# Forgetting attention and gated conv FFN on one core: a new written-out order for all engines, with the transposing loads in runs

## Chip, cores and metric

The kernel runs on one core of a Trainium2 chip. The metric is the device time of one execution in microseconds. The kernel before takes 264.0 us, the median of three runs (262.02 to 265.18).

## The reference

The inputs are q, k, v of shape (8, 8, 576, 64), that is batch, heads, sequence and head size, gates f of shape (8, 8, 576), and three weights. Cut to what matters:

```python
scores = scale * q @ k^T
decay  = cum[:, :, :, None] - cum[:, :, None, :]        # cum = cumsum(log(clip(f)))
attn   = softmax(where(causal, -1e9, scores + decay))
x      = (attn @ v), heads side by side                  # (8, 576, 512)
h      = relu(x @ w_in)                                  # (8, 576, 1024)
gate   = sigmoid(3-tap depthwise conv of h along the sequence)
out    = (h * gate) @ w_out                              # (8, 576, 512)
```

## The kernel before

**Attention.** The work goes by half batches of four heads, called hb, 16 of them. Two transposing DMAs (`load_qk`, line 172) bring k and q of one hb into one of four buffers `qk`, each value's two 16-bit halves in neighbouring partitions. The even partitions are then cleared of what isn't used and given rows for the decay: for hb 0 to 5 VectorE does it (`clamp`, line 182) and GpSimd starts small transfers of the rows (`own_rows`, `rows_of`, lines 188 to 199); from hb 6 two ordinary DMAs do both (`fill`, lines 205 and 207). TensorE then computes the scores in three kinds of task: `diag_scores` (diagonal blocks), `off_scores` (the blocks beside the diagonal, line 338) and `tail_scores` (the last 64 columns). ACT takes the exponential of each (`diag_exp`, `off_exp`, `tail_exp`, lines 383, 370, 350), GpSimd applies the causal mask on diagonal and tail blocks (lines 389, 353). `sums` and two `pv` tasks (line 406) give the row sums and the product with v; VectorE inverts the sums (`recip`, lines 414 to 416) and normalises into `xt` (`norm`, line 423).

**FFN.** For each of the 8 batches there are eight column blocks ff: `ffn1` on TensorE (line 433), `relu` on ACT (437), two conv steps on VectorE (443, 445), `tanh` on ACT (448), `gate` on VectorE (452). When all eight gates of a batch are there, `ffn2` (459, 464) multiplies with w_out, ACT copies the result out of PSUM (`evac`, 484) and SP stores it (492, 495). The last batch runs `ffn2_last` (473, 476), block by block as the gates come. FFN of one batch lies among the attention of later ones.

**Loads of ordinary kind.** `load_v` (line 249) brings v of a batch as five DMAs. w_in comes in four quarters (`load_in`, line 228), each cast to 16 bit by ACT (234) or VectorE (236). The first four ff blocks of a batch need the first two quarters only, the last four need all. w_out comes in four parts (`load_out`, 239). All of these, the transposing loads, the fills and the stores are issued by SP, in one order, and share one hardware queue.

**What sets the order.** Each piece is a task with an engine, a duration, the tasks it follows, and the buffers it takes and gives back (`Plan`, from line 12). The order of the tasks on each engine is written out by hand, as one string of letters per engine (`ORDER`, line 655; `KINDS`, line 647, says what a letter means; letters of one kind are taken in the order in which the tasks were added). `Plan.play` (line 36) walks through the five strings with the tasks' assumed durations, so as to merge them into one program order and to give each task its buffer. Buffers: four PSUM tiles `ps`, four `qk`, seven `pp`, two `vf` for v in 32 bit, three `ob` for results (line 112). A load into `qk` of hb n must follow the exponentials of hb n - 4.

The letters needed to follow the text: on TensorE d, o, t are diagonal, off-diagonal and tail scores, s sums, p pv, f ffn1, g and h ffn2, l and m ffn2_last. On VectorE k clamp, c the cast of w_in, r recip, n norm, a and b the conv steps, G gate, E evac. On SP y is load_v, j a quarter of w_in, J a part of w_out, q one transposing load (half of an hb), z fill, S store.

Of the kernel before, what the change touches and what calls it, by code (L numbers as in the profile page):

```python
# [18 lines left out]
class Plan:  # L19
# [11 lines left out]
    def add(self, kind, engine, time, after, fn, take=(), give=(), dma=0.0, small=False, lock=False):  # L31
        self.tasks.append(dict(kind=kind, engine=engine, time=time, after=list(after), fn=fn,
                               take=list(take), give=list(give), dma=dma, small=small, lock=lock))
        return len(self.tasks) - 1
# [50 lines left out]
def kernel(  # L85
# [93 lines left out]
    def clamp(hb, side, c0, c1):  # L179
        t = qk_t[hb % RING].bitcast(U16)[:, 0:2 * HS].rearrange("p (a x) -> p a x", a=2)  # L180
        t = t[:, :, c0:c1] if side is None else t[:, side, c0:c1]
        nc.vector.tensor_scalar(t, t, lim[:, 0:1], 0.0 if apart(hb, c0 // S) else lim[:, 1:2], op0=ALU.mult, op1=ALU.add)  # L182
# [18 lines left out]
    def fill(hb):  # L201
        c = slice(hb * HH, (hb + 1) * HH)
        none = image[3]
        nothing = bass.AP(tensor=none.tensor, offset=int(none.offset), ap=[[2 * S, 60], [1, 2 * HS]])
        nc.sync.dma_start(even_rows(hb, 8, 60, 0, 2 * HS),
                          nothing)
        nc.sync.dma_start(even_rows(hb, 0, 4, 0, 2 * HS).rearrange("j (a x) -> j a x", a=2),
                          image[:, :, c, :].rearrange("j a h s -> j a (h s)"))
# [43 lines left out]
    def cast_v(t_load, t_cast, hb, part, eng):  # L252
        vf, va = vf_t[slot[t_load, "vf"]][:, HH * (hb % 2):HH * (hb % 2 + 1)], va_t[slot[t_cast, "va"]]
        if part == 0:
            eng.tensor_copy(va[:, :, 0:4, :], vf[:, :, 0:4, :])  # L255
        else:
            eng.tensor_copy(va[0:SL, :, 4, :], vf[0:SL, :, 4, :])
# [87 lines left out]
    def tail_scores(me, hb):  # L345
        for h in range(HH):
            scores(ps_t[slot[me, "ps"]], SL * h, hb, h, 512, 512, SL, m=SL)
# [26 lines left out]
    def diag_scores(me, i):  # L374
        for x in range(WARM.get(i, 0) if i else 0):
            nc.tensor.matmul(ps_t[slot[me, "ps"]][:, 0:512], kc[:, 0:128], kc[:, 64:576], start=True, stop=True)
        for s in range(2):
            hb, h = where(i, s)
            for x, m in enumerate(DIAG):
                scores(ps_t[slot[me, "ps"]], 512 * (x // 2) + 256 * s + 128 * (x % 2), hb, h, 128 * m, 128 * m, 128)  # L380
# [48 lines left out]
    def ffn1(me, t_x0, ff):  # L429
        ps, xt = ps_t[slot[me, "ps"]], xt_t[slot[t_x0, "xt"]]  # L430
        for cc in range(NCC):
            for a in range(2):
                nc.tensor.matmul(ps[:, MB + 288 * a:MB + 288 * (a + 1)], w_in_f16[:, cc, 128 * ff:128 * (ff + 1)],  # L433
                                 xt[:, cc, 288 * a:288 * (a + 1)], start=(cc == 0), stop=(cc == NCC - 1))
# [19 lines left out]
    def ffn2(t_o, t_g0, c):  # L454
        ps, hg = ps_t[slot[t_o, "ps"]], hg_t[slot[t_g0, "hg"]]
        if c < 4:
            o = ps[:, 512 * (c % 2):512 * (c % 2 + 1)]
            for ff in range(NFF):
                nc.tensor.matmul(o, hg[:, ff, 128 * c:128 * (c + 1)], w_out_f16[:, ff, :],  # L459
                                 start=(ff == 0), stop=(ff == NFF - 1))  # L460
        else:
            for ff in range(NFF):
                for a in range(2):
                    nc.tensor.matmul(ps[64 * a:64 * (a + 1), 0:256], hg[:, ff, 512:576],  # L464
                                     w_out_f16[:, ff, 256 * a:256 * (a + 1)],
                                     start=(ff == 0), stop=(ff == NFF - 1), skip_group_check=True)
# [45 lines left out]
    for hb in range(NHB):  # L512
# [10 lines left out]
        if hb == 0:  # L523
# [5 lines left out]
            for y in range(2):  # L529
                for x in range(2):  # L530
                    e, d = (("ACT", 0.94), ("DVE", 0.6))[x]
                    t_win.append(add("cast_in", e, d, [t_win[2 * y + x]], lambda me, x=x, y=y, t_x=t_win[x]: cast_in(x, y, t_x),
                                     give=[(("vf", "hg")[x], t_win[x])] if y else [], lock=(e == "DVE")))
        if hb == 3:
            for w in range(4):
# [3 lines left out]
        e, eng, d = ("DVE", nc.vector, (0.7, 0.3)) if b == 0 else ("POOL", nc.gpsimd, (1.12, 0.5))  # L539
        x = add("cast_v", e, d[0], [t_vl[b]], lambda me, hb=hb, b=b, eng=eng: cast_v(t_vl[b], me, hb, 0, eng), take=["va"],  # L540
                lock=True)
# [6 lines left out]
        elif hb == 1:  # L548
            rows, most = [], []
            for s in (1, 0):  # L550
                x = add("clamp", "DVE", 0.46, [t_ld[hb, s]], lambda me, hb=hb, s=s: clamp(hb, s, 0, 2 * S), lock=True)
# [5 lines left out]
        elif hb < NCL:  # L557
            x = add("clamp", "DVE", 1.5, lands, lambda me, hb=hb: clamp(hb, None, 0, HS), lock=True)
            y = add("rows_of", "POOL", 1.2, [x, t_image], lambda me, hb=hb: rows_of(hb), small=True)
            rows = ([x, y],) * 2  # L560
        else:
            x = add("fill", "SP", 1.3, lands + [t_const, t_image], lambda me, hb=hb: fill(hb), dma=2.1)
            rows = ([x],) * 2
        for p in range(2):
            i = 2 * hb + p
            slow = ((3.0, 1.2)[p] if hb < 2 else 1.0)
            if p == (hb < 2):
                x = t_tail[hb] = add("tail_scores", "PE", (0.5 if hb < 2 else 0.2), rows[0] + rows[1], lambda me, hb=hb: tail_scores(me, hb),
                                     take=["ps", "pt"])
# [4 lines left out]
            x = t_dg[i] = add("diag_scores", "PE", 0.46 * slow, rows[p], lambda me, i=i: diag_scores(me, i),  # L574
                              take=["ps", "p"])
# [26 lines left out]
    for b in range(B):  # L602
        for ff in range(NFF):
            ready = [t_norm[4 * b + c] for c in range(4)] + t_win[4:6 if ff < 4 else 8]
            x = add("ffn1", "PE", 0.98, ready, lambda me, b=b, ff=ff: ffn1(me, t_x0[b], ff), take=["ps", "ht"],
                    give=[("xt", t_x0[b])] if ff == NFF - 1 else [])
# [10 lines left out]
        if b == B - 1:  # L617
# [7 lines left out]
            for a in range(3):  # L625
                e, d = (("ACT", 0.92), ("DVE", 1.2), ("ACT", 0.3))[a]
# [7 lines left out]
        for c in range(5):  # L634
# [3 lines left out]
            else:  # L638
                x = add("ffn2", "PE", 1.74, done, lambda me, t_o=t_o, g0=g0, c=c: ffn2(t_o, g0, c))
            t_f2 = x  # L640
            if c in (1, 3, 4):
# [5 lines left out]
    KINDS = {"w": "conv_weights", "d": "diag_scores", "o": "off_scores", "t": "tail_scores", "s": "sums",  # L647
             "p": "pv", "f": "ffn1", "g": "ffn2", "h": "ffn2_end", "l": "ffn2_last", "m": "ffn2_last_end",
             "D": "diag_exp", "O": "off_exp", "T": "tail_exp", "c": "cast_in", "R": "relu", "H": "tanh",
             "C": "cast_out", "E": "evac", "e": "evac_end", "k": "clamp", "W": "conv_ratios", "v": "cast_v",  # L650
             "V": "cast_v_end", "r": "recip", "n": "norm", "a": "conv", "b": "conv_end", "G": "gate",
             "x": "own_rows", "9": "own_row", "M": "diag_mask", "N": "tail_mask", "i": "decay_image",
             "X": "rows_of", "I": "constants", "y": "load_v", "j": "load_in", "q": "load_qk", "J": "load_out",
             "z": "fill", "S": "store"}
    ORDER = {
        "PE": "wdoodotodoosdotpopsppffffdoofdfofodtofdoostdpdopostoppoffffoggfdgtgosfdfopofohdtsdopppooffodfgfd"
              "gotsfffogogtdofppdosoopphodfffdfogtogsofpfofdgotdgpsoofppodftfodfhsfogogftppoffdfdgoosogoppshdof"
              "fdffhogfftogdfogfpdtgopsoopopdsdfofffophtpoffogsfgppgffgfffggfgfgfhfllllllllllllllllmmmmmmmm",
        "ACT": "DOOTODDOOODTOOcRRRHRcHDHOOHDRORODTRHOORHDHOCTDODOTOCHCRRCRORHOHHRDETHEOHRDROOROHeDTDHOHORORORDHH"
               "DRHTOEHRRORHOETDORHDOOOHOHReRDRDRHOHTOEHRORHORDOHDHTEOROHODRTRHODReRHOOHHTERHORRHDDROHHOOOHEeDRR"  # L660
               "DRRHOHOeRHHTRODHROERHDHTOEOOOHDDRORRHROHeTOHRROHREHHRHHRRHREHRERHRHEHRReHHHEe",
        "DVE": "kkWkkvvVVrnncrnnkabaaabbGGkGcbGabkababGranGnbrnnkGGaababGbaGaGbGbrGanbaabbrnnnGGaGabbabGaGbGabaG"
               "rabbnnaGrnbnGGGaabbabaGGbrGnaababGbGnrGnnGabaaGbbraaGbbGGnnaGbaaGbbarbGnGnGraababGaGbbaGbGabaGnb"
               "aGGnrbnnGrabaabbaGGnnGbaabraGnbnGbaGbGGabaGbaGbabGabGabGaaGbbGGE",
        "POOL": "x9MMNiMMNXXMMXNvVMMNvVMNMXIMvNVMvVMNMMMvNVvVMMNvvVVNMMMNMvvVNVMNMMMvvVVMNMMMNvVvVMNM",
        "SP": "yjjqqjqqjqqyJJqqJJqqyqzqqSzySqqzqyzSSqqSqzqyzqSqSSzqqSyzSqqSSzqqyzSSSSSSSSSSSS",
    }
    begin = {"EV": 0.0, "PE": 9.2, "ACT": 9.2, "DVE": 11.6, "POOL": 13.2, "SP": 13.5}
    for number in plan.play({e: [KINDS[x] for x in line] for e, line in ORDER.items()}, begin, 14.4, 6.5):
# [31 lines left out]
```

The softmax here doesn't subtract the row's maximum and nothing guards it: scores larger than these inputs give would overflow.

## Time and profile before

The profiled execution has a span of 265.7 us.

| engine | busy, us | share of the span |
|---|---|---|
| TensorE, matmul | 237.4 | 89% |
| TensorE, weight load | 154.0 | 58% |
| VectorE | 229.2 | 86% |
| ScalarE (ACT) | 203.0 | 76% |
| GpSimd (POOL) | 102.6 | 39% |

The DMA engines moved 49.28 MB, 48.00 MB of it on the one queue that SP fills. The profile's second part cuts the span into 40 equal slices and gives each engine's busy share of a slice in tenths. Its fourth part follows the chain of work that ended last back from the end, and says which engine and line held it for which share of the span; SPq stands for time in which SP issued a DMA. The timeline of SP lists each issue with its start and duration. The windows view gives, for a stretch of time, the busy time of TensorE, its weight loads, VectorE, ACT and POOL (with the number of instructions), then the granted clock of TensorE, the share of the DMA engines and what they moved in GB/s.

### The profile page before, as it was taken

What the parts mean: (1) busy time and instruction counts of PE and PEld (TensorE: products, weight loads), DVE (VectorE), ACT (ScalarE), POOL (GpSimd) and SP (SyncE); (2) the same over time, 40 slices, a digit from 0 to 9 for tenths busy, and PEclk for the clock granted to TensorE, in tenths of its full rate; (3) what the DMA queues carried; (4) which work ended last, traced back from release to release, by engine and by line L of the source; (5) the groups of instructions that cost most, each with busy time, mean ns of one, the idle gap of its engine ahead of it and who ended that gap; (6) DMA issues with size and microseconds to landing.
All of it is one profiled execution on the core that took longest, in us unless ns stands there. A gap on an engine that the chain in (4) does not pass through costs nothing.

```text
span 265.7 us, 7117 instructions
## 1 busy us (share of the span) xinstructions
PE 237.4 (89%) x2937; PEld 154.0 (58%) x2937; DVE 229.2 (86%) x327; ACT 203.0 (76%) x272; POOL 102.6 (39%) x145
## 2 busy tenths in 40 slices
PE   7979862987899997999799999998999999999991
PEld 2557542654565665746566576665766576565641
DVE  6547896678998998798999999999998999989971
ACT  4158465589988997889598998897799998557641
POOL 4248113256445750944705454347117913000000
PEclk9999999599999999999999999999999999999998
DMA  6999999999999999999999999999999920022414
GB/s 139 193 230 213 193 182 208 208 257 159 211 205 235 158 294 192 198 199 211 230 271 225 215 184 289 173 209 235 237 197 174 256 94 2 0 81 84 153 43 179
DMA packets 121895, 49.28 MB, mean 185 GB/s; under 512 B 113735, under 2 KB 114771, under 8 KB 121262
## 3 DMA queue, kind: packets, MB, share of 16 engines
q1 hardware_dynamic: 121078, 48.00, 90.7%
q0 software_dynamic: 704, 0.67, 0.8%
q8 instruction: 23, 0.38, 0.7%
q10 hardware_dynamic: 80, 0.15, 0.2%
q14 instruction: 10, 0.08, 0.2%
HBM read 19.89 MB, written 10.03 MB: 113 GB/s over the span
## 4 chain that ended last, share of the span: by engine, by line
PE 53%; DVE 17%; SPq 15%; ACT 5%; DMA 4%; issue 4%; POOL 0%; DVEq 0%; ACTq 0%; POOLq 0%
PE ps L433 17%; PE ps L459 14%; SPq L172 12%; PE ps L338 10%; PE ps L406 7%; DVE u L445 5%; DVE hg L452 4%; DVE u L443 3%; PE ps L473 3%; DVE xt L423 2%; DMA vf<-in_v_dram 2%; DMA hg<-in_moe_w_in_dram 2%; PE ps L464 2%; SPq L249 2%; ACT pp L370 2%
## 5 line engine op out<-in xcount | busy, mean ns | idle before, releaser
L433 PE MATMUL ps<-xt,w_in_f 128*128 128x288 f16 x512 | 72.5, 290 | 6.9 <-DVE w_in_f L236 4.6
L338 PE MATMUL ps<-qk 128*128 128x128 bf16 (+2 forms) x576 | 63.0, 242 | 11.6 <-DVE u L445 2.6
L370 ACT ACTIVATE pp<-ps 128x1024 f16<-128x1024 f32 x64 | 64.7, 1029 | 5.9 <-PE ps L338 4.4
L389 POOL TENSOR_SCALAR_AFFINE_SELECT pp<-pd 128x512 f16<-128x512 f32 x64 | 50.5, 814 | 47.1 <-ACT pd L383 47.0
L433 PEld LDWEIGHTS <-w_in_f 128*128 128x128 f16 x512 | 49.5, 99 | 23.0 <-DVE w_in_f L236 4.9
L443 DVE SCALAR_TENSOR_TENSOR u<-ht,cwt 128x576 f32<-128x576 f16 x64 | 53.0, 838 | 8.8 <-ACT ht L437 8.5
L448 ACT ACTIVATE hg<-u,cw 128x576 f16<-128x576 f32 x64 | 49.6, 781 | 12.5 <-DVE u L445 12.3
L445 DVE SCALAR_TENSOR_TENSOR u<-ht,cwt,u 128x576 f32<-128x576 f16 x64 | 57.8, 916 | 0.5
L452 DVE SCALAR_TENSOR_TENSOR hg<-hg,ht 128x576 f16<-128x576 f16 x64 | 55.0, 871 | 2.6 <-ACT hg L448 1.9
L338 PEld LDWEIGHTS <-qk 128*128 128x128 bf16 x576 | 38.8, 99 | 28.6 <-issue 9.1
L437 ACT ACTIVATE ht<-ps 128x576 f16<-128x576 f32 x64 | 41.8, 657 | 17.1 <-PE ps L433 15.6
L459 PE MATMUL ps<-w_out_f,hg 128*128 128x512 f16 x224 | 52.5, 379 | 0.0
L383 ACT ACTIVATE pd<-ps 128x1024 f32<-128x1024 f32 x32 | 32.9, 1032 | 10.3 <-PE ps L343 6.2
L459 PEld LDWEIGHTS <-hg 128*128 128x128 f16 x224 | 21.3, 98 | 21.2
L353 POOL TENSOR_SCALAR_AFFINE_SELECT pt<-p 128x256 f16<-128x256 f32 x16 | 11.7, 734 | 38.9 <-ACT p L350 38.1
L423 DVE TENSOR_TENSOR xt<-ps,rb 128x576 f16<-128x576 f32 x32 | 23.3, 749 | 3.6 <-PE ps L406 3.2
L406 PE MATMUL ps<-pp,va 128*32 128x128 f16 (+2 forms) x768 | 25.8, 274 | 0.2 <-ACT p L350 0.2
L406 PEld LDWEIGHTS <-va 128*32 128x32 f16 x896 | 18.1, 96 | 10.1 <-issue 4.7
L484 ACT COPY ob<-ps 128x1024 f32<-128x1024 f32 (+1 forms) x23 | 18.3, 796 | 6.0 <-PE ps L473 1.9
L255 POOL CAST va<-vf 128x1024 f16<-128x1024 f32 x14 | 17.5, 1266 | 2.6 <-DMA vf<-in_v_dram 2.4
L406 PE MATMUL ps<-pp,ones_h 128*32 128x128 f16 (+2 forms) x384 | 13.7, 274 | 0.8 <-DVE xt L423 0.4
L182 DVE TENSOR_SCALAR qk<-qk,lim 128x1152 uint16<-128x1152 uint16 (+2 forms) x10 | 9.6, 979 | 5.4 <-DMA qk<-in_q_dram 3.4
(87 smaller groups left out, 170.1 us busy)
## 6 DMA issues: line engine op xcount, KB each, us to landing
vf<-in_v_dram SPq DMA_DIRECT2D x32, 256.0 KB, 4.8
out_dram<-ob SPq DMA_DIRECT2D x16, 512.0 KB, 4.5
qk<-image SPq DMA_DIRECT2D x10, 540.0 KB, 5.7
ob<-in_moe_w_out_dram SPq DMA_DIRECT2D x4, 512.0 KB, 6.8
vf<-in_v_dram SPq DMA_DIRECT2D x8, 128.0 KB, 5.5
vf<-in_moe_w_in_dram SPq DMA_DIRECT2D x2, 512.0 KB, 6.6
hg<-in_moe_w_in_dram SPq DMA_DIRECT2D x2, 512.0 KB, 5.5
out_dram<-ob SPq DMA_DIRECT2D x16, 64.0 KB, 4.0
```

The costliest lines, as they stand in the source:

```text
L338: nc.tensor.matmul(o, tk[:, h * S + k0:h * S + k0 + 128], tq[:, h * S + q0:h * S + q0 + n], start=True, stop=not apart(hb, h))
L370: nc.scalar.activation(blocks(t_dg)[:, 2 * s:2 * s + 2, 128:640], ps_t[slot[t_sc, "ps"]].rearrange("p (a c) -> p a c", a=2), AF.Exp, scale ...
L383: nc.scalar.activation(pd_t[slot[me, "pd"]], ps_t[slot[t_dg, "ps"]], AF.Exp, scale=SCALE)
L389: nc.gpsimd.affine_select(to, pd[:, x], pattern=[[0, 4], [1, 128]], base=0, channel_multiplier=-1, compare_op=ALU.is_ge, fill=0.0)
L406: nc.tensor.matmul(ps[32 * h:32 * (h + 1), AB + q0:AB + q0 + n], left_of(h, m), p, start=x in (0, 1), stop=x in (0, 6), skip_group_check=True)
L433: nc.tensor.matmul(ps[:, MB + 288 * a:MB + 288 * (a + 1)], w_in_f16[:, cc, 128 * ff:128 * (ff + 1)], xt[:, cc, 288 * a:288 * (a + 1)], sta ...
L437: nc.scalar.activation(ht_t[slot[t_m1, "ht"]][:, 1:1 + S], ps_t[slot[t_m1, "ps"]][:, MB:MB + S], AF.Relu, scale=0.5)
L443: nc.vector.scalar_tensor_tensor(u, ht[:, 0:S], cwt[:, ff, 0:1], ht[:, 1:1 + S], op0=ALU.mult, op1=ALU.add)
L445: nc.vector.scalar_tensor_tensor(u, ht[:, 2:2 + S], cwt[:, ff, 1:2], u, op0=ALU.mult, op1=ALU.add)
L448: nc.scalar.activation(hg_t[slot[t_g0, "hg"]][:, ff, :], u_t[slot[t_u, "u"]], AF.Tanh, scale=cw[:, ff, 1:2])
L452: nc.vector.scalar_tensor_tensor(hv, hv, 1.0, ht_t[slot[t_m1, "ht"]][:, 1:1 + S], op0=ALU.add, op1=ALU.mult)
L459: nc.tensor.matmul(o, hg[:, ff, 128 * c:128 * (c + 1)], w_out_f16[:, ff, :], start=(ff == 0), stop=(ff == NFF - 1))
```

## The change

Only the strings in `ORDER` are new (two tables of letters change places in `KINDS`, which has no effect). Every letter occurs as often as before, so all instructions stay. The new strings come from a search in which the replay of the schedule knows whether the DMA ahead of a DMA was a transpose or an ordinary one, and charges for the change from one kind to the other. It is for a DMA stream with fewer such changes: in the SP string the q stand in 9 runs, before in 17. The orders of the other four engines were searched anew with it. The durations that `Plan.play` uses are left as they were.

```diff
     ORDER = {
-        "PE": "wdoodotodoosdotpopsppffffdoofdfofodtofdoostdpdopostoppoffffoggfdgtgosfdfopofohdtsdopppooffodfgfd"
-              "gotsfffogogtdofppdosoopphodfffdfogtogsofpfofdgotdgpsoofppodftfodfhsfogogftppoffdfdgoosogoppshdof"
-              "fdffhogfftogdfogfpdtgopsoopopdsdfofffophtpoffogsfgppgffgfffggfgfgfhfllllllllllllllllmmmmmmmm",
+        "PE": "wdoodtodooosdtooppsppffffdtdooodftooffsdoootpdpfdsopopoofffdsfgogftfgodgfpofdoptosdhooppodffffod"
+              "gogffsogdofogtppstfdoppoohdtfffsfodgogfoptfdgoopfgosfddppotofdffohsoogtfdppfogffdoospgoofpsdgftf"
+              "fodfohhogfgppofdotsfofdppgofogfdsofftdofppooghsfgfppfgfgfffgghfggffflllllllllllllllmmlmmmmmm",
...
-        "DVE": "kkWkkvvVVrnncrnnkabaaabbGGkGcbGabkababGranGnbrnnkGGaababGbaGaGbGbrGanbaabbrnnnGGaGabbabGaGbGabaG"
...
-              "aGGnrbnnGrabaabbaGGnnGbaabraGnbnGbaGbGGabaGbaGbabGabGabGaaGbbGGE",
-        "POOL": "x9MMNiMMNXXMMXNvVMMNvVMNMXIMvNVMvVMNMMMvNVvVMMNvvVVNMMMNMvvVNVMNMMMvvVVMNMMMNvVvVMNM",
-        "SP": "yjjqqjqqjqqyJJqqJJqqyqzqqSzySqqzqyzSSqqSqzqyzqSqSSzqqSyzSqqSSzqqyzSSSSSSSSSSSS",
+        "DVE": "WkkkkvvVVrcnnrnnkabaabkGGbaGkcbabGarGanbnbkarnnGbGaGbaabaGbGabbGarGGnabbanrbnnGGGaaabbbGGabGraba"
...
+              "GbnnaGbaGGbarGaabbnnaGbGrGabbnnaGbaGbGGaabaGbabbGabGGGabaaGbbGGE",
+        "POOL": "Mx9MNMiMNXXNMXMMvNVvMVXNMMIvMNVMvVMvNMVMvMVNMvvNMVNVMMMNvvVMVNMMMNvMvMVVNMvMNMVMNMvV",
+        "SP": "yjjqqqqqqjjyJJqqyJJqqqqzyzqqqqSzSyzSqqqqSzzySSqqqSzySqqqSzSqSzqSyzSSSSSSSSSSSS",
     }
```

## The prediction, made before the change was run

> **What bounds the kernel now.** I read the page first (busy shares, slices, chain), then the timeline of the SP queue, then windows of the trace. Busy shares and slices:
>
> ```profile
> PE 237.4 (89%) x2937; PEld 154.0 (58%) x2937; DVE 229.2 (86%) x327; ACT 203.0 (76%) x272; POOL 102.6 (39%) x145
> PE   7979862987899997999799999998999999999991
> DVE  6547896678998998798999999999998999989971
> DMA  6999999999999999999999999999999920022414
> ```
>
> A slice is 6.6 us. From slice 11 (73 us) both TensorE and VectorE are at 8 or 9 nearly everywhere: the later three quarters of the kernel are bound by two engines at once. The visible hole is slice 6 (40 to 47 us), where TensorE is at 2. The DMA engines are full until slice 32 (about 212 us). The chain of waits by line says what the early part hangs on:
>
> ```profile
> PE 53%; DVE 17%; SPq 15%; ACT 5%; DMA 4%; issue 4%; POOL 0%; DVEq 0%; ACTq 0%; POOLq 0%
> ```
>
> Nearly all of the 15% of SPq and half of the 4% of DMA lie before 45.7 us: the chain in order of time runs through SP issues up to 40.24 us, then 5.47 us of "DMA hg<-in_moe_w_in_dram", then a VectorE cast. After that DMA comes up once (5.77 us at 97.10). The SP queue in that stretch (start, duration, engine, line, operation):
>
> ```profile
> 13.54 4.98 SPq L249 DMA_DIRECT2D vf<-in_v_dram  x5
> 18.56 0.63 SPq L228 DMA_DIRECT2D vf<-in_moe_w_in_dram  x1
> 19.24 0.61 SPq L228 DMA_DIRECT2D hg<-in_moe_w_in_dram  x1
> 19.89 6.53 SPq L172 DMA_TRANSPOSE qk<-in_k_dram  x1
> 26.46 4.16 SPq L172 DMA_TRANSPOSE qk<-in_q_dram  x1
> ...
> 31.30 6.03 SPq L172 DMA_TRANSPOSE qk<-in_k_dram  x1
> 37.37 2.83 SPq L172 DMA_TRANSPOSE qk<-in_q_dram  x1
> 40.24 0.59 SPq L228 DMA_DIRECT2D hg<-in_moe_w_in_dram  x1
> 41.03 4.79 SPq L172 DMA_TRANSPOSE qk<-in_k_dram  x1
> 45.92 2.99 SPq L172 DMA_TRANSPOSE qk<-in_q_dram  x1
> ```
>
> A transpose that follows an ordinary transfer holds the queue longer (6.53, 6.03, 4.79) than one that follows a transpose (4.16, 2.83, 2.99). Over the whole timeline after 13.5 us there are 17 of the first kind, mean 4.6, and 11 of the second, mean 3.2 us. Windows of 1 us show where it goes (the last columns are granted clock, DMA share, GB/s):
>
> ```profile
> 34.00:35.00 1.00, 1.00 (x11) 0.79 (x9) 1.00 (x2) 0.68 (x2) 0.00 (x0) 1.00 1.27 280
> 35.00:36.00 1.00, 1.00 (x11) 0.80 (x9) 0.96 (x2) 0.68 (x2) 0.71 (x2) 1.00 2.46 128
> 36.00:37.00 1.00, 1.00 (x9) 0.66 (x7) 1.00 (x2) 0.81 (x2) 0.32 (x1) 1.00 0.06 8
> 37.00:38.00 1.00, 0.92 (x5) 0.19 (x2) 1.00 (x3) 1.00 (x3) 0.00 (x0) 1.00 1.08 242
> ```
>
> Between the quarter of w_in issued at 30.67 and the transpose behind it the stream almost stops for some 1.5 us (128, then 8 GB/s). So the switch has a cost on this chip, and the change is aimed at something real. Whether it is on the path is the question.
>
> What is left to gain on TensorE after the hole (PE busy is the second number group):
>
> ```profile
> 47.00:75.00 28.00, 23.70 (x320) 16.23 (x321) 23.06 (x28) 24.07 (x31) 14.32 (x22) 0.91 1.13 209
> 95.00:115.00 20.00, 17.69 (x229) 12.00 (x228) 17.05 (x22) 16.47 (x23) 11.50 (x13) 1.00 1.13 228
> 115.00:135.00 20.00, 17.92 (x268) 12.02 (x267) 18.21 (x26) 16.05 (x21) 9.02 (x11) 1.00 1.01 213
> 210.00:252.00 42.00, 41.72 (x488) 26.79 (x487) 39.87 (x58) 30.84 (x44) 5.96 (x9) 1.00 0.22 79
> ```
>
> TensorE idle is 4.30, 2.31, 2.08 and 0.28 us in these four; the windows between them leave 0.29 (75 to 95), 0 (135 to 156), 1.41 (156 to 185) and 0.41 (185 to 210). Together 11.1 us of 205. The waits view names the start of it and the one DMA wait in it:
>
> ```profile
> PE ps L433 <- DVE w_in_f L236: 4.6, 1, 4.6
> PE ps L338 <- DMA vf<-in_v_dram: 1.3, 1, 1.3
> ```
>
> **What the Trainium skill says.** "Perfetto Trace Analysis", section "DMA Instruction — HWDGE (DVE, Sync)": the reported window of a DMA issue covers getting and using the descriptor generator, not the semaphore wait ahead of it and not the movement of the data. The trace agrees: the issue at 40.24 took 0.59 us and its data landed 5.47 us later. So 6.53 us of a transpose is queue back-pressure, not a wait for data it needs. "DMA: Bandwidth & Descriptors", section "Latency and other measured facts": a DMA transpose moves 261 GB/s. One load here is 4 heads of 576 rows of 256 B, 590 KB, so 2.3 us; the shortest in the trace that follows a transpose is 2.16 us. "Perfetto Trace Analysis", section "Identifying the Most-Contended Engine": matmul busy time overstates how full TensorE is, and weight loads are to be looked at; here they are at 58%. So TensorE's 9s can hide a little slack, which speaks against treating 237 us as hard. I rely on no page for the price of the switch; it is from the trace.
>
> **The change part by part.** No instruction is added or removed, so all busy sums stay. What moves:
>
> (1) *Fewer switches.* In the SP string the q letters form 17 runs before and 9 after. Eight switches less, at 4.6 - 3.2 = 1.4 us, is 11 us of queue time out of about 195. It lies beside compute, except where a DMA ends a wait: up to 45.7 us, and the 1.3 us at 103 us.
>
> (2) *The opening.* Before, the last quarter of w_in (the fourth j) stands behind four loads, after it behind six, and both late quarters follow the run. To 30.6 us the two SP orders are the same. Then four transposes in a run: the two in-run issues of this stage took 2.83 and 2.99, so 4 x 2.9 = 11.6, to 42.2; the last j is issued at 42.8 and, with the 5.47 us of before, lands at 48.3 instead of 45.7: **2.6 us later**. Bounds: with 2.2 us each (the shortest) it lands at 45.5, with 3.2 (the mean) at 49.5. Who waits: the second VectorE cast (c), behind it on VectorE a conv_end and gates, and on TensorE the fifth f. But the new TensorE order has d t d o o o d ahead of that f where the old has d o o d: one d, one t and one o more, by the rows of the timeline about 0.55 + 0.3 + 0.55 = 1.4 us, and VectorE has one more clamp (1.48 us) ahead of c. The hole is filled by that much: net **+1.2 us** at this point (-1.4 to +2.4).
>
> (3) *What comes back from it.* The loads of the third and fourth batch halves land earlier: the last q of hb 4 leaves the queue at 42.2 instead of 48.9. From 47 to 75 us TensorE and VectorE lack 4.3 and 4.9 us, in small waits on ACT results and on each other; with more score work ready there is more to place in them. V loads also stand earlier (third y ahead of the second pair of J), so I take the DMA wait of **1.3 us** at 103 us as gone.
>
> (4) *The rest of the reordering.* 9.75 us of TensorE idle are left (11.1 less 1.3), ended by the latency of score, exp, mask and of relu, conv, tanh, gate. The profile cannot show what a new interleaving does with it. Bounds: nothing, or all. I take a third, **-3.3 us**, because VectorE itself is at 190 of 205 us in the same stretch, so that not all can go.
>
> (5) *Edits with no cost or gain.* conv_ratios ahead of the clamps on VectorE fills part of its 1.94 us wait for the k load before 13.49; diag_mask ahead of own_rows on POOL ends at about 14.8, when own_rows started before anyway. At the end the old order has g, f, h, f before ffn2_last, the new one three f in a row. The last f then still needs relu, a, b, tanh and gate with two other f: gates of the last three end some 5.3 us after the last f, and the seventh pair of ffn2_last needs the last of them about 6.0 us after it (14 x 0.43). The chain of before has those 32 matmuls back to back (6.91 us), so nothing changes: 0.
>
> Sum: 264.0 + 1.2 - 1.3 - 3.3 = **260.6 us**.
>
> **The rivals.** *Hidden anyway:* after 47 us almost nothing waits for DMA, so the saved 11 us are worth the 1.3 us only, the opening eats them, and the new interleaving is no better than the old one. 264.0 + 1.2 - 1.3, and half a us either way: 263.5 us. For it speaks the chain (53% PE, 17% DVE, and DMA once after 45.7), against it the 11.1 us of idle. *Slower:* the run costs 2.4 us in the opening, and later runs of four put fills, v loads and stores behind two more transposes (2 x 2.9 = 5.8 us) on a queue that goes in order; if half of one such delay reaches TensorE, 264.0 + 2.4 + 2.9 - 1.3 = 268 us. For it speaks that run loads need free qk buffers (four), against it that only one late wait for DMA is seen now. *Larger gain:* the opening costs nothing and 70% of the idle goes: 264.0 - 1.3 - 6.8 = 256 us. VectorE near its limit speaks against it.
>
> **How the numbers follow.** Chances: forecast 0.45, hidden 0.28, slower 0.18, larger gain 0.09. About 0.85 of the forecast's case lies under 261.4 (1% faster), with the larger gain and a little of "hidden" that is 0.51; slower over 266.6 is most of the slower case and a little of the rest, 0.18; within 1% 0.31. The range goes from the larger gain, 256.0, to just inside the slower case, 267.5.
>
> **What would show it.** In the new profile: in-run transposes at about 2.9 us; the last w_in quarter landing near 48 us, and the wait of L433 on w_in_f still there but smaller than 4.6; the span's DMA stream ending earlier than 210 us, by up to 11 us; no wait of L338 on a DMA near 100 us; TensorE idle after 50 us near 6.5 instead of 11.1. Wrong if in-run transposes are no shorter, if PE waits for qk or v behind a run, or if idle after 50 us is as large as before.

## The result, and the profile after

| | before | changed | ratio (95% interval) |
|---|---|---|---|
| median time, us | 263.01 (261.14 to 265.18) | 271.76 (270.96 to 273.16) | 1.036 (1.027 to 1.045) |

The change makes the kernel 8.7 us slower, where 3.4 us less had been forecast; the time lies above the whole range given, 256.0 to 267.5. In what follows, the comparison is mostly with a second profile of the unchanged kernel, **the unchanged kernel again** (262.39 us, span 260.7), because the profile shown before the prediction was taken in an execution of 267.45 us, some 4 us over the kernel's median. The profiled execution of the changed kernel has a span of 271.4 us. Its busy shares, its slices (6.8 us each, counted from 0; PEclk is the granted clock in tenths) and its chain by engine:

```profile
PE 241.1 (89%) x2935; PEld 156.5 (58%) x2937; DVE 230.5 (85%) x327; ACT 203.8 (75%) x272; POOL 100.8 (37%) x145
PE   7959695878989599989999999994999999999992
DVE  6726789888989759989999999995699999999881
PEclk9999989799999979999999999997799999999997
PE 45%; DVE 22%; SPq 15%; DMA 9%; ACT 5%; issue 3%; DVEq 0%; ACTq 0%
```

To the hole at 40 to 47 us that TensorE had before, two later ones have come, slice 13 (88 to 95 us) and slice 27 (183 to 190 us), and VectorE falls with TensorE or just after it. There the clock shows a 7 (slice 14; slices 27 and 28); the 7 of slice 7 belongs to the opening, where the clock falls in both kernels. The DMA share of the chain has gone from 4 to 9%; 4 of the 9 are the two late fills. The largest entry among the waits of TensorE (total, times, longest) names the two holes:

```profile
PE ps L338 <- DMA qk<-image: 6.8, 2, 3.4
```

`qk<-image` is the fill of a half batch's even partitions (lines 205 and 207). TensorE's timeline has both places; at the end of a line, in brackets, the idle time ahead of it:

```profile
93.16 1.06 PE L338 MATMUL ps<-qk 128*128 128x128 bf16 x12 [3.38 <-DMA qk<-image]
187.85 1.04 PE L338 MATMUL ps<-qk 128*128 128x128 bf16 x8 [3.44 <-DMA qk<-image]
188.68 3.62 PE L459 MATMUL ps<-w_out_f,hg 128*128 128x512 f16 x8
```

The first is hb 6, the second hb 13. Eight matmuls of line 459 took 3.62 us just behind the second wait; in the unchanged kernel again such a group of eight took 1.89. Windows show why (third number from the end: granted clock):

```profile
93.00:96.00 3.00, 2.84 (x47) 1.88 (x48) 0.76 (x2) 2.10 (x3) 1.01 (x2) 0.74 1.32 217
96.00:98.00 2.00, 2.00 (x32) 1.04 (x31) 0.27 (x1) 1.53 (x3) 0.22 (x1) 0.54 1.34 213
188.00:191.00 3.00, 3.00 (x14) 1.59 (x13) 0.27 (x1) 1.69 (x2) 0.90 (x2) 0.50 0.93 201
191.00:194.00 3.00, 3.00 (x18) 1.64 (x16) 2.67 (x4) 1.08 (x2) 1.53 (x3) 0.59 0.00 0
```

The Trainium skill, "TensorE: Matmul & The Clock Gate", section "HAM oscillation — how this bites in real kernels", says that idle gaps of TensorE over about 3.4 us make the clock fall to half. The two waits here are about that long, 3.38 and 3.44 us, and 5 and 6 us at 0.5 to 0.74 follow them. But 3.4 us is no limit in this case. In a run below (both fixes and the fills moved) one wait of 1.84 us in an otherwise full stretch is followed by 4 us at 0.59:

```profile
112.14 1.14 PE L433 MATMUL ps<-xt,w_in_f 128*128 128x288 f16 x8 [1.84 <-ACT pd L383]
113.00:117.00 4.00, 3.56 (x38) 1.81 (x36) 3.90 (x6) 2.86 (x4) 1.90 (x2) 0.59 0.89 265
```

In another (only the fill of hb 13 moved) a wait of 2.25 us, 57.6 to 59.9, is followed by no fall. So the clock depends on more than the length of one wait, and each late fill here costs its wait once and then again in slow matmuls: (1 - 0.74) x 3 + (1 - 0.54) x 2 = 1.7 us at the first and (1 - 0.50) x 3 + (1 - 0.59) x 3 = 2.7 us at the second, with VectorE short of work in three of the four windows.

Against the unchanged kernel again, the span grew by 10.7 us. TensorE's busy time rose from 236.5 to 241.1, **4.6 us**, which the slow clock explains (1.7 + 2.7 = 4.4; in the first 75 us the clock costs either kernel about 3.4 us, an estimate made in the same way from windows of 1 us); its idle time rose from 24.2 to 30.3, **6.1 us**, and the two waits are 6.8. That accounts for the loss in the profile. The chain in order of time (start, length) goes through the same two places:

```profile
82.16 1.61 SPq L172
83.86 3.07 SPq L172
87.10 6.01 DMA qk<-image
...
177.49 3.43 SPq L172
183.19 4.61 DMA qk<-image
```

Why the fills are late stands in SP's timeline of the changed kernel, first hb 6, then hb 13:

```profile
68.72 5.41 SPq L172 DMA_TRANSPOSE qk<-in_k_dram  x1
74.22 6.53 SPq L172 DMA_TRANSPOSE qk<-in_q_dram  x1
80.91 2.86 SPq L172 DMA_TRANSPOSE qk<-in_k_dram  x1
83.86 3.07 SPq L172 DMA_TRANSPOSE qk<-in_q_dram  x1
87.10 0.97 SPq L205 DMA_DIRECT2D qk<-image  x1
...
174.74 2.70 SPq L172 DMA_TRANSPOSE qk<-in_k_dram  x1
177.49 3.43 SPq L172 DMA_TRANSPOSE qk<-in_q_dram  x1
181.01 1.18 SPq L495 DMA_DIRECT2D out_dram<-ob  x2
182.28 0.86 SPq L205 DMA_DIRECT2D qk<-image  x1
```

and in that of the unchanged kernel again, for the same two:

```profile
76.61 3.85 SPq L172 DMA_TRANSPOSE qk<-in_k_dram  x1
80.57 0.96 SPq L205 DMA_DIRECT2D qk<-image  x1
...
168.43 4.33 SPq L249 DMA_DIRECT2D vf<-in_v_dram  x5
172.80 0.86 SPq L205 DMA_DIRECT2D qk<-image  x1
```

The fill of hb 6 is issued at 87.1 instead of 80.6 us, that of hb 13 at 182.3 instead of 172.8. Ahead of the first stand two transposes of a later hb (2.86 + 3.07 us) and one held for 6.53 us; ahead of the second two transposes and a store (2.70 + 3.43 + 1.18 = 7.3 us). The transposes of a run go out together, and a fill that belongs to the first of them waits for the last two.

The runs didn't shorten the queue either. From 13 us on, by kind of issue on SP (times summed from the timelines; idle only where SP stands for more than 0.2 us; the last column is the run below that has only the new SP order):

| SP, us | before, first profile | before again | changed | new SP order alone |
|---|---|---|---|---|
| transposes (28) | 113.6 | 108.7 | 104.0 | 101.9 |
| v loads (8) | 43.0 | 39.6 | 50.0 | 50.7 |
| idle ahead of the last fill | 2.2 | 2.0 | 6.4 | 0.8 |
| last fill issued at | 206.8 | 200.9 | 208.2 | 202.9 |

### The profile page after: what moved, and what is told of

Same layout as the page of the kernel before. It is cut to its first block, busy times and chain, and to the rows that moved or that the text cites. A ratio compares the mean times of both kernels' runs of the same rounds, so it can differ in the third digit from the quotient of the medians.

```text
span 271.4 us, 7122 instructions
## 1 busy us (share of the span) xinstructions
PE 241.1 (89%) x2935; PEld 156.5 (58%) x2937; DVE 230.5 (85%) x327; ACT 203.8 (75%) x272; POOL 100.8 (37%) x145
## 4 chain that ended last, share of the span: by engine, by line
PE 45%; DVE 22%; SPq 15%; DMA 9%; ACT 5%; issue 3%; DVEq 0%; ACTq 0%
PE ps L433 14%; SPq L172 12%; PE ps L459 12%; PE ps L338 8%; PE ps L406 6%; DVE u L445 6%; DVE hg L452 5%; DVE u L443 5%; DMA qk<-in_q_dram 5%; DMA qk<-image 4%; PE ps L473 3%; PE ps L464 2%; ACT pp L370 2%; SPq L249 2%; DVE xt L423 2%
## 5 line engine op out<-in xcount | busy, mean ns | idle before, releaser
L338 PE MATMUL ps<-qk 128*128 128x128 bf16 (+2 forms) x576 | 62.3, 245 | 15.8 <-DMA qk<-image 6.8
L389 POOL TENSOR_SCALAR_AFFINE_SELECT pp<-pd 128x512 f16<-128x512 f32 x64 | 51.8, 833 | 63.7 <-ACT pd L383 56.4
L443 DVE SCALAR_TENSOR_TENSOR u<-ht,cwt 128x576 f32<-128x576 f16 x64 | 57.1, 903 | 4.2 <-ACT ht L437 3.6
L452 DVE SCALAR_TENSOR_TENSOR hg<-hg,ht 128x576 f16<-128x576 f16 x64 | 54.0, 854 | 7.6 <-ACT hg L448 7.0
L338 PEld LDWEIGHTS <-qk 128*128 128x128 bf16 x576 | 39.5, 100 | 32.2 <-issue 8.0
L459 PE MATMUL ps<-w_out_f,hg 128*128 128x512 f16 x224 | 54.3, 388 | 1.6 <-DVE st L414 1.4
L255 POOL CAST va<-vf 128x1024 f16<-128x1024 f32 x14 | 17.1, 1227 | 13.4 <-DMA vf<-in_v_dram 11.6
L353 POOL TENSOR_SCALAR_AFFINE_SELECT pt<-p 128x256 f16<-128x256 f32 x16 | 10.5, 658 | 20.9 <-ACT p L350 18.3
L414 DVE STREAM_TRANSPOSE st<-ps 128x576 f32<-128x576 f32 x16 | 12.4, 773 | 3.0 <-PE ps L406 2.9
L406 PE MATMUL ps<-pp,ones_h 128*32 128x448 f16 (+2 forms) x384 | 14.2, 283 | 0.2 <-ACT ht L437 0.2
## 6 DMA issues: line engine op xcount, KB each, us to landing
vf<-in_v_dram SPq DMA_DIRECT2D x32, 256.0 KB, 5.8
```

The source lines that it names most:

```text
L338: nc.tensor.matmul(o, tk[:, h * S + k0:h * S + k0 + 128], tq[:, h * S + q0:h * S + q0 + n], start=True, stop=not apart(hb, h))
L389: nc.gpsimd.affine_select(to, pd[:, x], pattern=[[0, 4], [1, 128]], base=0, channel_multiplier=-1, compare_op=ALU.is_ge, fill=0.0)
L406: nc.tensor.matmul(ps[32 * h:32 * (h + 1), AB + q0:AB + q0 + n], left_of(h, m), p, start=x in (0, 1), stop=x in (0, 6), skip_group_check=True)
L443: nc.vector.scalar_tensor_tensor(u, ht[:, 0:S], cwt[:, ff, 0:1], ht[:, 1:1 + S], op0=ALU.mult, op1=ALU.add)
L452: nc.vector.scalar_tensor_tensor(hv, hv, 1.0, ht_t[slot[t_m1, "ht"]][:, 1:1 + S], op0=ALU.add, op1=ALU.mult)
```

## The experiments

Theories at the start. **A:** the fills of hb 6 and 13 come late behind runs, constants and stores, and TensorE waits (two waits, and the clock behind them). **B:** the new orders of the compute engines are worse by themselves. **C:** the switch between kinds costs nothing on this queue, so that runs bring nothing and the rest of the reordering decides.

### The old SP order in the changed kernel, and the new one in the old kernel

```diff
 # changed kernel, SP order of before
-        "SP": "yjjqqqqqqjjyJJqqyJJqqqqzyzqqqqSz...
+        "SP": "yjjqqjqqjqqyJJqqJJqqyqzqqSzySqqz...
```

> The changed kernel with the old order of the SP queue and the four new compute orders. Theory A (late fills: TensorE waits 3.4 us at 89.8 and 3.4 us at 184.4 for the fill DMAs of hb 6 and 13, because of where the new SP order puts them, and then runs at a low clock): both waits shrink, but the new TensorE order needs the fourth batch half early and the old queue brings it late, so 265 to 269 us. Theory B (the new compute orders are worse by themselves): it stays at 270 to 274 us with no large DMA wait in it. Theory C (the fewer changes of DMA kind are what costs, whatever the rest): 262 to 264 us.

Measured: 270.96 us, ratio 1.029 (1.022 to 1.035). SP's timeline in this run, and a line of GpSimd's:

```profile
184.61 0.40 SPq L492 DMA_DIRECT2D out_dram<-ob  x1
191.24 1.19 SPq L495 DMA_DIRECT2D out_dram<-ob  x2
...
202.21 5.59 SPq L249 DMA_DIRECT2D vf<-in_v_dram  x5
```

```profile
210.94 1.30 POOL L255 CAST va<-vf 128x1024 f16<-128x1024 f32 x1 [18.53 <-DMA vf<-in_v_dram]
```

The old SP order asks for a store of results (line 495) that the new compute orders make later. SP stands from 185.0 to 191.2 us; v of the last batch, behind it in the order, is issued at 202 and GpSimd waits 18.5 us. From 210 to 230 us TensorE is then idle for 3.5 us, against 0.1 in the unchanged kernel again. So the two strings must fit each other. The time lies above the 265 to 269 us of A and in the range of B, and TensorE itself waits for no DMA longer than 1.4 us after the opening: this run alone doesn't rule B out.

```diff
 # kernel before, SP order of the changed kernel
-        "SP": "yjjqqjqqjqqyJJqqJJqqyqzqqSzySqqz...
+        "SP": "yjjqqqqqqjjyJJqqyJJqqqqzyzqqqqSz...
```

> The kernel before with only the new SP order. Theory A (each SP order fits only the compute orders that it was searched with; a mismatch makes TensorE wait behind an in-order queue): slower, 266 to 275 us, with TensorE waits on w_in or on fills and stores that hold up the queue. If the runs of transposes save queue time by themselves, as the prediction had it: under 264 us.

Measured: 268.49 us, ratio 1.020 (1.017 to 1.024). TensorE's timeline:

```profile
47.55 1.14 PE L433 MATMUL ps<-xt,w_in_f 128*128 128x288 f16 x4 [7.32 <-ACT w_in_f L234]
51.70 1.14 PE L433 MATMUL ps<-xt,w_in_f 128*128 128x288 f16 x4 [3.01 <-DVE w_in_f L236]
```

With the old TensorE order the late quarters of w_in cost 10.3 us of waiting, and the clock is at 0.50 from 47 to 54 us. Runs alone don't help. In the changed kernel the wait for w_in is 0.69 us, but with another of 3.08 us just ahead of it.

### The two late fills, one at a time and together

The three constants (`constants`, lines 216 to 218) are written to DRAM by GpSimd's own queue, at 69.7 to 71.4 us in the changed kernel, just ahead of the 6.53 us transpose. One edit issues them four letters earlier, one takes the fill of hb 13 ahead of a transpose and a store.

```diff
-  POOL  ...MVXNMMIvMNV...       # constants: letter I
+  POOL  ...MVIXNMMvMNV...
```

> The changed kernel; on GpSimd the three constants transfers are issued before the clamp rows of hb 5 instead of after three masks, so some 8 us earlier, beside the v load. Theory A, first half (the constants slow the transposes of hb 6 to 6.53 us, so its fill is late): the wait at 89.8 us falls from 3.4 to under 1 us and the low clock after it goes, 266 to 269 us. Theory B: no change in time, 270 to 273 us. If the constants have no part in it: the second transpose of the run stays over 5 us and the wait stays.

```diff
-  SP    ...SzySqqqSzSqSz...     # fill of hb 13: the second z
+  SP    ...SzySqqzqSSqSz...
```

> The changed kernel; on the SP queue the fill of hb 13 is issued one transpose and one small store earlier (about 4.6 us). Theory A, second half: the wait at 184.4 us falls from 3.4 to under 1 us, the clock stays full in 185 to 210, and the time falls by the wait and some 2 us of low clock, 265 to 268 us. Theory B: 270 to 273 us.

> The changed kernel with both moves (constants earlier, fill of hb 13 earlier). Theory A: both waits of 3.4 us and both stretches of low clock are gone; 6.8 us of waits and 3 to 4 us of clock, so 260 to 263 us, level with or under the kernel before. Theory B: over 268 us.

| | us | ratio to before (95% interval) | waits of L338 on `qk<-image`: us, longest |
|---|---|---|---|
| changed | 271.76 | 1.036 (1.027 to 1.045) | 6.8, 3.4 |
| constants earlier | 270.13 | 1.023 (1.016 to 1.030) | 6.3, 3.1 |
| fill of hb 13 earlier | 267.80 | 1.015 (1.008 to 1.021) | 2.4, 1.4 |
| both | 266.06 | 1.009 (1.006 to 1.012) | 4.2, 1.6 |

With the constants earlier the slow transpose is gone and the fill of hb 6 leaves at 84.28 instead of 87.10; the time of this edit alone can't be told from that of the changed kernel, since the intervals overlap. With the fill of hb 13 moved they don't. With both, SP and TensorE at hb 6 (SP lines, then the TensorE line):

```profile
73.96 3.34 SPq L172 DMA_TRANSPOSE qk<-in_q_dram  x1
83.65 0.95 SPq L205 DMA_DIRECT2D qk<-image  x1
```

```profile
89.69 1.04 PE L338 MATMUL ps<-qk 128*128 128x128 bf16 x12 [1.17 <-DMA qk<-image]
```

After the opening no wait brings the clock down any more (1.00 in each window from 75 to 210 us). Against the runs of before that go with each, the loss falls from 8.7 us to 2.3 (266.06 against 263.78). So most of the loss is late fills, as A says, though A expected 260 to 263 us and so all of it.

How much of this is due to the constants isn't shown. The delay of the transpose goes with them: the second transpose of hb 6 took 6.53, 4.82 and 6.06 us in three profiles with the constants in their old place, and 3.33, 3.34 and 3.45 in three with them moved. But the wait of TensorE at hb 6 is not the same in each execution: in the profile with only the fill of hb 13 moved, whose order is that of the changed kernel up to there, it is 0.52 us.

### Is the switch between kinds dear at all?

Kernels with nothing but the DMAs on SP and a store of zeros; all compute is left out. First eight transposes and eight v loads, in turn, or in two runs, without and with the constants' writes on GpSimd's queue at the start of one run or of the other:

```diff
 # the order in which SP issues, q transpose, y v load
-  qyqyqyqyqyqyqyqy
+  qqqqqqqqyyyyyyyy
```

> DMA only, no attention and no FFN: 8 transposing loads of 590 KB and 8 loads of v (1.18 MB each in five transfers), taken in turn, into buffers of their own; then one small store. 15 changes of kind. If a change of kind costs 1.4 us as the step in the prediction had it: about 10 to 20 us longer than the same loads in two runs. If the longer issue after an ordinary load is only back-pressure of the load ahead: within 3 us of the two runs.

> The same DMA-only loads, all 8 transposes first, then all 8 v loads: one change of kind. At the 200 to 230 GB/s of the kernel's stream 14.2 MB take 62 to 71 us, plus about 10 us ahead and after.

> As the two runs, transposes first, with the three constants transfers issued by GpSimd at the start, beside the transposes. If these small transfers slow transposes down (in the changed kernel the stream fell to some 100 KB per us for 6 us): 3 to 6 us longer than the two runs without them, with one transpose issue over 5 us. If not: under 1.5 us longer.

> The two runs in the other order, v loads first, with the constants at the start, beside the v loads. If the slowing is special to transposes: within 2 us of the two runs without constants. If it comes with any stream: 3 to 6 us longer, too.

Measured: in turn 69.96 us, in runs 70.97, in runs with the constants beside the transposes 70.87, beside the v loads 70.91. So between transposes and v loads there is **no switch cost** to save, as far as one execution of each can tell. Within the alternation a transpose holds the queue 3.15 to 3.39 us after a v load, against 2.0 to 2.9 in the run, but the v loads then take 4.4 to 5.1 us instead of 43.49 / 8 = 5.4: a long issue shows when the queue has room again, not what its own transfer costs. And beside transposes alone the constants cost nothing.

Then the other partners, in blocks of four and four: quarters of w_in (j) and fills (z), in turn and in runs.

```diff
+  qjqjqjqj qqqqjjjj qzqzqzqz qqqqzzzz
```

> DMA only, no attention and no FFN, in four blocks one after the other: 4 transposes and 4 quarters of w_in in turn, then in runs; 4 transposes and 4 large fills (60 rows of 9216 B) in turn, then in runs. With v loads the order made no difference (69.96 against 70.97 us). If a change of kind costs where the ordinary transfer has large packets (2048 or 9216 B), as the gap of 1.5 us behind a quarter of w_in suggests: the blocks in turn are 4 to 10 us longer than their runs. If not: within 1.5 us.

SP's timeline (in turn with w_in, run, in turn with fills, run); the first line stands behind the constants' writes, which GpSimd issues at 2 to 4 us here:

```profile
10.32 4.74 SPq L131 DMA_TRANSPOSE qk<-in_q_dram  x1
15.74 4.77 SPq L131 DMA_TRANSPOSE qk<-in_k_dram  x1
21.19 4.94 SPq L131 DMA_TRANSPOSE qk<-in_q_dram  x1
26.18 2.68 SPq L131 DMA_TRANSPOSE qk<-in_k_dram  x1
...
36.52 6.61 SPq L131 DMA_TRANSPOSE qk<-in_q_dram  x1
43.25 0.94 SPq L142 DMA_DIRECT2D fl<-image  x1
44.24 4.46 SPq L131 DMA_TRANSPOSE qk<-in_k_dram  x1
64.74 2.33 SPq L131 DMA_TRANSPOSE qk<-in_k_dram  x1
```

In turn, a transpose and a w_in quarter take 5.43 us together (issues at 10.32, 15.74, 21.19), four pairs 21.7. Eight in runs (three transposes, four quarters, one transpose) pass from 26.18 to 43.25, 17.1 us. The difference, 4.65 us, is for three switches back and forth: **about 1.55 us for each**. So C falls in part: behind quarters of w_in the cost is real, and close to the 1.4 us that the prediction read off the trace; behind v loads it isn't there. In turn with fills the transposes hold the queue nearly as long as with w_in (4.4 to 4.5 us); what a switch costs there was not worked out.

### Taking load off the queue in both kernels

Here v loads from the fourth batch on bring only the last 64 rows; the rest of v in the buffer is stale. Fills and transposes stay.

```diff
-        for kb in range(NKB):
+        for kb in range(NKB) if b < 3 else (NKB - 1,):
```

> The changed kernel with four fifths of the v loads left out from the fourth batch on (only the last 64 rows of v are loaded, so the output of these batches is not the reference's); some 5 MB less on the queue after 87 us. Theory A (the deliveries of the in-order queue come too late for the new TensorE order): the wait for the fill of hb 13 at 184 us and the low clock after it go, the wait for hb 6 at 90 us stays (it stands ahead of the first light load): 264 to 267 us. Theory B (the compute orders are slower by themselves): 269 us or more.

> The kernel before with the same v loads left out (same loss of output). Theory A: its queue delivers in time, apart from w_in, so it gains little: 261 to 263.5 us. If the DMA stream holds up the kernel before as well: under 260 us.

Measured: the changed kernel 263.81 us, ratio 1.001 (0.998 to 1.003) to the whole kernel before; the kernel before with the same edit 262.70, ratio 1.000 (0.997 to 1.004). The lighter queue gives the changed kernel 8 us and the kernel before nothing. So B falls, as far as the whole of the loss goes: once deliveries aren't late, the new compute orders are within about 1 us of the old. In the profile of the changed kernel with this edit (an execution of 267.92 us, at the upper end of its times) the hb 13 wait is gone; hb 6 comes before the first cut v load, and its wait is there:

```profile
93.23 1.89 PE L338 MATMUL ps<-qk 128*128 128x128 bf16 x12 [3.27 <-DMA qk<-image]
```

Whether the executions near the median have that wait too isn't known.

### Two tries at a better order

On top of both fixes, the fill of hb 6 one transpose earlier, and that of hb 7 straight behind its own pair and ahead of the v load:

```diff
-  SP    ...JJqqqqzyz...
+  SP    ...JJqqqzqzy...
```

> The changed kernel with the constants and the fill of hb 13 moved as before, and the fills of hb 6 and 7 also earlier (the first one transpose earlier, the second ahead of the v load). Theory A: the two waits left of 1.2 and 1.4 us on these fills go, and 1 to 2 us of time with them: 264 to 265.5 us. If the rest over the kernel before comes from the compute orders: no change, 266 us.

Measured: 268.65 us, ratio 1.021 (1.018 to 1.023), where it was 1.009 without it. The fill of hb 7 has to wait for the transpose just ahead of it to land: SP is free at 87.10 and issues the fill at 89.13. The v load behind it leaves at 90.71 instead of 85.60, and GpSimd waits 5.30 us for v at 100.82. Putting one delivery forward put another back. Two waits of TensorE at 60 and 69 us (2.04 and 2.35 us) precede the moved fills and aren't explained by them, so not all of the 1.2% is due to the moved fills.

And in the kernel before, the last quarters of w_in ahead of two pairs of transposes:

```diff
-  SP    yjjqqjqqjqqyJJ...
+  SP    yjjqqjjqqqqyJJ...
```

> The kernel before; on the SP queue the last quarter of w_in goes ahead of two transposes (y jj qq jj qqqq), all other orders kept. The wait of TensorE for w_in (3.8 and 4.6 us in two profiles, near 46 us) is the largest single one; the quarter should land near 40 instead of 44 to 46 us, the third batch half 2 to 3 us later, which TensorE needs only at about 50 us. If that wait is on the path: 260 to 262 us. If the search had placed the loads at their best: 263 us or more, with the wait moved to the transposes of hb 3 or 4.

Measured: 262.35 us, ratio 0.999 (0.997 to 1.002). The wait for w_in shrinks from 3.76 us (the unchanged kernel again) only to 2.86, and a new one of 1.16 us of line 338 on `qk<-image` appears at 42.08. No order that was tried is faster than the kernel before.

The unchanged kernel again, used for comparison throughout:

> The kernel before, unchanged: a second profiled execution of it, for a trace nearer to its median (the profiled execution shown was 267 us, the median of 23 runs is 263.8). Both theories: about 262 to 265 us, with the same waits; some of the 11 us of TensorE idle after 47 us that the prediction counted should be smaller.

Measured: 262.39 us. TensorE idle from 47 us on, over the same windows as in the prediction, is 7.9 us up to 210, where the profile of before had 10.8, and there is no wait for a DMA near 100 us.

## Why the prediction was wrong

Two terms failed: the third of the idle in step 4, which no wait backed, and the delay of the fills behind the runs, which the sum had at nothing and only a rival counted.

**Step 4, a third of the idle comes back (-3.3 us), failed, and it failed with the wrong sign.** From 47 to 210 us TensorE's idle went from 7.9 us in the unchanged kernel again (10.8 in the first profile) to 15.2 in the changed one. Two windows hold most of it, here the unchanged kernel again and then the changed one:

```profile
75.00:95.00 20.00, 19.84 (x284) 12.75 (x286) 19.02 (x26) 18.57 (x27) 10.45 (x12) 1.00 1.10 221
185.00:210.00 25.00, 24.59 (x336) 15.95 (x335) 23.59 (x32) 23.60 (x32) 13.02 (x14) 1.00 1.00 227
```

```profile
75.00:95.00 20.00, 15.42 (x147) 9.16 (x149) 16.76 (x23) 14.72 (x21) 7.42 (x9) 0.99 1.13 187
185.00:210.00 25.00, 22.15 (x242) 14.59 (x243) 18.55 (x26) 17.41 (x25) 4.90 (x7) 0.86 0.84 191
```

TensorE idle goes from 0.16 to 4.58 us and from 0.41 to 2.85. These are just the stretches that the prediction passed over as nearly full (0.29 and 0.41 there). The third was a choice with nothing under it: the profile of before said how much idle there is, not that the new orders would find it. The prediction also counted idle from an execution some 4 us over the median, and so had more to gain than there was.

**Step 1, eight switches less at 1.4 us, counted one side of an exchange.** Against the profile it was worked out from, transposes did take less of the queue, 9.6 us of the 11 (4.7 against the unchanged kernel again), but v loads took 7.0 more (10.4) and SP stood idle 6.4 us instead of 2.2 up to the last fill, which left 1.4 us later (7.3 later than in the unchanged kernel again). The two profiles of the unchanged kernel differ by 5.9 us in this, so a small gain could not be seen; 11 us would be. The run with only the new SP order shows the same exchange (101.9 and 50.7 us). In the old order six of the eight v loads stand straight behind a transpose, in the new one two. The DMA-only runs show the exchange by itself: in turn, a transpose is longer by about as much as the v load behind it is shorter. The mean over 17 issues, 4.6 against 3.2 us, took the first half of that for a cost of each switch. But this is not the whole account. By the letters, only one of the eight switches that went stood behind a v load; two stood behind quarters of w_in, where a real cost was measured, four behind fills and one behind a store. Why these bring nothing on the whole isn't shown.

**Step 2, the opening: the landing was right, the filling of the hole was not.** The last quarter of w_in was issued at 42.94 (42.8 forecast) and its cast could start at 48.95, forecast 48.3:

```profile
48.95 0.69 DVE L236 CAST w_in_f<-hg 128x1024 f16<-128x1024 f32 x1 [0.53 <-DMA hg<-in_moe_w_in_dram]
```

The wait of line 433 on w_in fell to 0.69 us. But the scores that were put ahead of it had to wait themselves. First the changed kernel, then the unchanged one again:

```profile
47.76 0.61 PE L338 MATMUL ps<-qk 128*128 128x128 bf16 x8 [3.08 <-DVE hg L452]
49.06 1.47 PE L433 MATMUL ps<-xt,w_in_f 128*128 128x288 f16 x8 [0.69 <-ACT w_in_f L234]
...
46.13 1.13 PE L433 MATMUL ps<-xt,w_in_f 128*128 128x288 f16 x4 [3.76 <-DVE w_in_f L236]
```

3.08 + 0.69 = 3.77 us: the hole is as large as before. The gate on VectorE that is named had ended 0.7 us earlier; a transfer of decay rows, issued by GpSimd at 42.70 (line 199), took 5.0 us to land, and the weight load of these scores starts just then, at 47.73. Up to 75 us TensorE is idle for 14.0 us against 15.1 in the unchanged kernel again, so the +1.2 us of this step isn't seen. With the old TensorE order the new SP order costs 10.3 us of waiting here, so the new interleaving does make up for the later quarters.

**Step 3, the DMA wait of 1.3 us at 103 us gone:** gone, but it is also absent from the unchanged kernel again, so there was nothing to gain.

**Step 5, nothing at the start and the end:** for the start no figure was taken; it was right for the end: from 210 us to its last matmul TensorE has no gap worth counting in either kernel (49.99 us busy of the 50 from 210 to 260 in the changed one).

**The rival "slower" (chance 0.18, 268 us) had the mechanism.** It named fills behind two more transposes, 2 x 2.9 = 5.8 us on an in-order queue; measured, 2.86 + 3.07 us at hb 6 and 2.70 + 3.43 at hb 13. It let half of one such delay reach TensorE, 2.9 us. In fact it happened twice, 3.4 us each, and each brought the clock down, 4.4 us more that neither the sum nor the rival had. What spoke against the rival, "only one late wait for DMA is seen now", was the old order's merit and no property of the queue. The signs listed as "wrong if" all came: in-run transposes no shorter (3.2 us in both), TensorE waiting for qk behind a run, and more idle.

**What stays open.** The delay of the transpose at 74.22 (6.53 us) goes when the constants move, and the waits put it down to their landing; but constants beside transposes in the DMA-only run cost nothing, so how they slow it here isn't settled. Why v loads behind fills and stores hold the queue longer (5.6 to 7.8 us, against 4.7 and 5.4 behind a transpose) isn't settled either. The last 2.3 us of the version with both fixes weren't located.

## What to carry to other kernels

The order of a DMA queue and the orders of the engines are one schedule: price a reordered queue at each consumer, by asking for every transfer that now stands behind others when its reader needs it, and not by the queue time saved. A wait of TensorE can cost more than its length: behind those of 3.38 and 3.44 us the slow clock took 1.7 and 2.7 us more. Before counting idle time as a gain, look at whether the profile is of a typical execution, and give no share of it to an order whose waits haven't been followed.

## What the hardware showed that was not expected

- A change between a transposing and an ordinary transfer on one queue cost about 1.55 us for each switch back and forth beside the 2048-byte rows of w_in, and nothing beside the 256-byte rows of the v loads (69.96 us in turn, 70.97 in runs). The loads differ in size too (0.5 and 1.18 MB), and each figure is from one execution, so that the rows are the reason isn't shown.
- In a run with nothing else, a transpose of 590 KB takes 2.0 to 2.9 us of the queue; within the full kernel 19 in-run transposes took 3.2 us on average.
- The clock of TensorE fell to 0.59 for 4 us behind a wait of only 1.84 us, and stayed at 1.00 behind one of 2.25 us in another run.
- One store in the wrong place of an in-order queue held it for 6.2 us (185.0 to 191.2) and made another engine wait 18.5 us, 20 us later.
